# Eight more attention units transposed outside TensorE, and the whole instruction order as one list

## The chip, the cores and the metric

The kernel runs on one NeuronCore of one Trainium2 chip. The metric is the device time of one execution in microseconds (us), as a median of runs. The engines go by the profile's names: PE is TensorE (matmul), PEld its weight loads, DVE is VectorE, ACT is ScalarE, POOL is GpSimd, SP issues most of the DMAs. They share nothing but memory and semaphores; each runs its own instructions strictly in the order in which they stand in the program.

## What is computed

Banded attention with a linear bias, and behind it a layer whose activation is a ratio of two polynomials, all in float32 (8 batches, 8 heads, 576 positions, 64 numbers per head; 4608 tokens of 512 numbers, 2048 hidden numbers):

```python
scores = scale * np.matmul(q, k.transpose(0, 1, 3, 2))
...
mask = (rel >= 0) & (rel < window)          # window = 128
scores = np.where(mask, scores + bias[None], -1000000000.0)
scores = scores - np.max(scores, axis=-1, keepdims=True)
attn = np.exp(scores)
attn = attn / (np.sum(attn, axis=-1, keepdims=True) + 1e-09)
return np.matmul(attn, v)                   # becomes x
...
h = x @ w_in
P = a[0] + a[1] * h + a[2] * h2 + a[3] * h3
Q = 1.0 + np.abs(b[0]) * np.abs(h) + np.abs(b[1]) * h2
g = P / (Q + 1e-6)
return g @ w_out
```

## The kernel before

**The layer.** The 36 blocks of 128 tokens form 18 tiles of two blocks. A tile goes through the 16 chunks of 128 hidden numbers, two chunks at a time: the up matmuls (L980) fill one PSUM bank `h`, a chain on ACT, POOL and DVE (L1008 to L1026) turns `h` into `g`, split into a high part `g_h` (a cast on ACT) and the rest `g_l` (a subtraction on DVE, L1026, the last reader of `h`), and the down matmuls (L1044) add `g_h` and `g_l` times the weights into two banks `acc`. To keep float32 accuracy every product is made of three: high times high, low times high, high times low. So nearly all PE time is in six kinds of matmul. There are three `h` banks; an up group can start only when the bank that it takes has been released.

**The attention.** 76 units, each two heads and one or two blocks of a tile, four units for each later tile. A unit's matmuls stand in a *session* on PE between matmuls of the layer: the scores of unit u (L558), and the probabilities times `v` of unit u-2 (L694), whose result goes into two banks, `px` (one of the three banks that `h` uses too) and `py`. ACT then copies `px` away (`x<-px`, a copy that shows as line L387) and DVE adds `py` (L707); a cast and a subtraction (L709, on DVE or POOL) make `x_hi` and `x_lo`. Between scores and values stands the softmax: DVE (L567, L574), ACT (L579), POOL (L621). The values need the probabilities transposed, key by query. Two ways exist:

- *On PE*: `turn_halves` transposes them with eight matmuls (L604) at the head of the next session, three copies (L651, L652) bring them back to SBUF, and two affine selects on POOL (L658) cut them into the two sides of the band.
- *Through HBM*: `cross`: one DVE instruction (L629) transposes all the 32 by 32 squares of the 128 by 512 probabilities, one DMA writes them to HBM (`z_dram`), four DMAs read them back with the squares in their new places, and two affine selects on POOL (L636) cut them. Units from `CROSS` up to the last but two go this way.

**What sets the order.** Every piece of work is an `Op` with a due time, the engines that can run it and a cost. `Plan.order` puts them into one list: first the codes in `FIRST` one by one (number of the op, plus 10000 if its second possible engine is to run it), then a greedy choice among the ops that are ready by the plan's own estimate of times. The list is only an order: on the chip semaphores decide when each instruction starts. In the kernel before, `FIRST` has 1370 codes of 6486 ops; the greedy choice makes the rest, from about 60 us on.

Of the kernel before, what the change touches and what calls it, by code (L numbers as in the profile page):

```python
# [11 lines left out]
F32 = mybir.dt.float32  # L12
# [8 lines left out]
P = 128  # L21
# [318 lines left out]
def banded_attention_ratio_mlp(ctx: ExitStack, tc: tile.TileContext, kqv, w_in, w_out, ab, bias, ident, out):  # L340
# [22 lines left out]
    CROSS, CT, CM = 24, 2.27, 0.744  # L363
# [5 lines left out]
    def slot(pool, shape, dtype, name, tag=None, view=None):  # L369
        return Slot(pool, count[id(pool)], shape, dtype, name, tag or name, view)  # L370

    def ap(s):
        if s.ap is None:
            s.ap = s.pool.tile(s.shape, s.dtype, name=s.name, tag=s.tag)
        return s.ap
# [134 lines left out]
    class Unit:  # L510
# [112 lines left out]
        def cross(self):  # L623
            u, A, m, n, pr = self.u, self.A, self.m, self.n, self.pr
            z = slot(const, [P, 4, n, 32], F32, "z", tag=("spare0", "part")[u % 2])
            d = slot(dr4, [P, 4, n, 32], F32, "z_dram")
            x = slot(const, [P, 4, n, 32], F32, "x_turn", tag=("raw", "w1")[u % 2])
            w = self.w = slot(sb2, [P, 2, 4 * n, 32], F32, "p_all")
            plan.op(A + CT, {"v": 69 + 1.042 * n * P}, lambda e: nc.vector.transpose(ap(z).rearrange("q k y c -> q (k y c)"), ap(pr).rearrange("q y c -> q (y c)")), reads=[(pr, y) for y in range(n)], writes=[(z, 0)], follows=([*(y[0] for y in heads.values())], [parts[1]])[u % 2] if u < CROSS + 2 else (), sb=True)  # L629
            plan.op(A + CT, {"s": 728}, lambda e: eng[e].dma_start(ap(d), ap(z)), reads=[(z, 0)], writes=[(d, 0)])  # L630
            for k in range(4):
                r = slice(32 * k, 32 * k + 32)
                plan.op(A + CT, {"s": 182}, lambda e, k=k, r=r: eng[e].dma_start(ap(x)[r], ap(d)[:, k].rearrange("(g a) y c -> a g (y c)", a=32)), reads=[(d, 0)], writes=[(x, k)])
            cost = {"g": 135 + 0.93 * n * P}
            for k, sign in ((1, 1), (0, -1)):
                plan.op(A + CM - 0.1 * k, cost, lambda e, k=k, sign=sign: nc.gpsimd.affine_select(  # L636
                    out=ap(w)[:, k].rearrange("q (g y) c -> q g y c", g=4), in_=ap(x), pattern=[[32 * sign, 4], [0, n], [sign, 32]], compare_op=ALU.is_ge, fill=0.0, base=k - 1, channel_multiplier=-sign), reads=[(x, j) for j in range(4)], writes=[(w, k)])
# [73 lines left out]
    def attention(u):  # L711
# [25 lines left out]
        if u > CROSS and not turned:  # L737
            cost += 70
# [440 lines left out]
```

## Time and profile before

| what | value |
|---|---|
| three runs | 980.14, 982.7, 983.0 us; median 982.7 |
| the profiled execution's own time | 981.46 us |
| its span, first to last instruction | 979.7 us |
| granted TensorE clock, mean | 0.999 of 2.4 GHz |
| busy share: PE, PEld, DVE, ACT, POOL | 99%, 86%, 82%, 68%, 56% |
| mean DMA rate | 97 GB/s |

A busy PE says only that some matmul was under way: matmuls are pipelined, and each record (0.28 us for 256 columns) overlaps the next, which starts 0.12 us later. A stall shows best as the distance between the starts of two matmuls that follow each other.

### The profile page before, as it was taken

How to read it: one execution, taken by the hardware profiler on the slowest of the kernel's cores; microseconds unless marked ns; L12 is line 12 of the kernel's file. 1: busy time of each engine (PE TensorE's matmuls, PEld its weight loads, DVE VectorE, ACT ScalarE, POOL GpSimd, SP SyncE). 2: the span in 40 equal slices, each digit the busy share in tenths (PEclk: the TensorE clock that was granted, in tenths of full speed). 3: DMA queues.
4: the chain of work that ended last, by engine and by line, in shares of the span. 5: the costliest groups of instructions: out<-in, count | busy, mean ns of one | idle time of the engine just before them, and what ended most of it. 6: DMA issues, size and time to landing. Idle time of an engine off the chain costs nothing.

```text
span 979.7 us, 24224 instructions
## 1 busy us (share of the span) xinstructions
PE 971.1 (99%) x9029; PEld 840.7 (86%) x9031; DVE 806.6 (82%) x1929; ACT 666.8 (68%) x1567; POOL 549.3 (56%) x626
## 2 busy tenths in 40 slices
PE   9999999999999999999999999999999999999998
PEld 5767898888988888888888888888888888888997
DVE  5999988877878787978887888888887978886775
ACT  6999776676766666666666666666676666666563
POOL 3898965555655555645555454556555555454332
PEclk9999999999999999999999999999999999999999
DMA  8963212112323222323232322323232323210000
GB/s 278 364 234 127 90 52 67 44 66 71 114 93 124 68 96 87 115 73 103 96 103 85 108 94 78 125 67 120 84 101 79 114 79 99 73 53 23 1 23 22
DMA packets 81142, 95.30 MB, mean 97 GB/s; under 512 B 8448, under 2 KB 59264, under 8 KB 81024
## 3 DMA queue, kind: packets, MB, share of 16 engines
q1 hardware_dynamic: 80736, 93.49, 28.6%
q8 instruction: 71, 1.16, 0.5%
q14 instruction: 47, 0.39, 0.1%
q10 hardware_dynamic: 288, 0.26, 0.1%
HBM read 71.18 MB, written 22.54 MB: 96 GB/s over the span
## 4 chain that ended last, share of the span: by engine, by line
PE 87%; DVE 5%; DMA 3%; ACT 2%; issue 1%; SPq 1%; POOL 0%; ACTq 0%; DVEq 0%
PE h L980 39%; PE acc L1044 39%; PE sc L558 4%; PE px L694 3%; DMA raw_w<-in_w_in 2%; DMA kq<-in_kqv 1%; DVE g_p L1012 1%; DVE g_l L1026 1%; ACT g_p L1010 1%; DVE h L1018 1%; DMA raw_w<-in_w_out 1%; PE py L694 1%; DVE w L906 0%; ACT g_u L1008 0%; DVE g_q L1017 0%
## 5 line engine op out<-in xcount | busy, mean ns | idle before, releaser
L980 PE MATMUL h<-x_hi,wi_hi 128*128 128x256 f32 x1024 | 291.9, 285 | 2.4 <-DVE g_l L1026 2.3
L980 PE MATMUL h<-x_lo,wi_hi 128*128 128x256 f32 x1024 | 287.6, 281 | 0.0
L980 PE MATMUL h<-x_hi,w_lo 128*128 128x256 f32 x1024 | 287.3, 281 | 0.0
L1009 POOL TENSOR_SCALAR g_q<-g_u,babs 128x512 f32<-128x512 f32 x142 | 109.4, 770 | 216.9 <-ACT g_u L1008 211.8
L980 PEld LDWEIGHTS h<-x_lo,wi_hi 128*128 128x128 f32 x1024 | 192.6, 188 | 35.2
L1044 PE MATMUL acc<-wo_hi,g_h 128*128 128x512 f32 x548 | 221.8, 405 | 0.0
L980 PEld LDWEIGHTS h<-x_hi,wi_hi 128*128 128x128 f32 x1024 | 192.9, 188 | 33.4 <-issue 14.0
L1044 PE MATMUL acc<-w_lo,g_h 128*128 128x512 f32 x548 | 216.2, 395 | 0.0
L1044 PE MATMUL acc<-wo_hi,g_l 128*128 128x512 f32 x548 | 208.6, 395 | 0.0
L980 PEld LDWEIGHTS h<-x_hi,w_lo 128*128 128x128 f32 x1024 | 193.6, 189 | 0.0
L1011 POOL TENSOR_TENSOR g_q<-g_q,g_u 128x512 f32<-128x512 f32 x143 | 184.8, 1293 | 13.9 <-DVE g_q L1009 2.9
L1017 DVE SCALAR_TENSOR_TENSOR g_q<-g_q,h 128x512 f32<-128x512 f32 x144 | 98.5, 684 | 77.0 <-ACT h L1016 75.1
L1014 ACT ACTIVATE g_u<-g_q,guard 128x512 f32<-128x512 f32 x144 | 104.2, 724 | 81.8 <-POOL g_q L1011 81.8
L1008 ACT ACTIVATE g_u<-h 128x512 f32<-128x512 f32 x141 | 84.2, 597 | 82.0 <-PE h L980 81.9
L621 POOL TENSOR_TENSOR pr<-pr,st 128x512 f32<-128x512 f32 (+1 forms) x76 | 75.7, 996 | 107.9 <-DVE st L590 32.4
L387 ACT CAST g_h<-h 128x512 fp32r<-128x512 f32 x134 | 78.6, 586 | 69.1 <-DVE h L1024 62.7
L1012 DVE TENSOR_TENSOR g_p<-h,g_p 128x512 f32<-128x512 f32 x144 | 98.7, 685 | 30.7 <-ACT g_p L1010 30.2
L579 ACT ACTIVATE pr<-pr,st 128x128 f32<-128x128 f32 x288 | 113.5, 396 | 15.1 <-DVE st L574 12.2
L1044 PEld LDWEIGHTS acc<-wo_hi,g_h 128*128 128x128 f32 x548 | 103.1, 188 | 7.8 <-issue 1.2
L1026 DVE TENSOR_TENSOR g_l<-h,g_h 128x512 fp32r<-128x512 f32 x137 | 94.0, 686 | 17.8 <-ACT g_h L387 16.3
L1010 ACT ACTIVATE g_p<-h,na 128x512 f32<-128x512 f32 x140 | 108.6, 776 | 0.0
L1013 DVE SCALAR_TENSOR_TENSOR g_p<-g_p,na,h 128x512 f32<-128x512 f32 x144 | 106.8, 741 | 1.7
(112 smaller groups left out, 1761.3 us busy)
## 6 DMA issues: line engine op xcount, KB each, us to landing
kq<-in_kqv SPq DMA_DIRECT2D x68, 320.0 KB, 3.3
v<-in_kqv SPq DMA_DIRECT2D x68, 192.0 KB, 2.8
z_dram<-z SPq DMA_DIRECT2D x50, 256.0 KB, 2.0
x_turn<-z_dram SPq DMA_DIRECT2D x200, 64.0 KB, 2.0
out<-o SPq DMA_DIRECT2D x34, 256.0 KB, 2.0
raw_w<-in_w_in SPq DMA_DIRECT2D x16, 512.0 KB, 6.6
raw_w<-in_w_out SPq DMA_DIRECT2D x16, 512.0 KB, 6.2
bias_t<-in_bias SPq DMA_DIRECT2D x44, 64.0 KB, 2.4
```

The lines of the kernel that those rows point to most:

```text
L579: nc.scalar.activation(self.row(y), self.row(y), AF.Exp, bias=ap(st)[:, y : y + 1], scale=-1.0, accum_out=ap(st)[:, 4 + y : 5 + y])
L980: nc.tensor.matmul(h(i), w[:, k, :], x[:, k, :], start=(k == 0 and m == 0), stop=(k == NKC - 1 and m == len(seq) - 1))
L1008: plan.op(E, either(soon, act(W, 1), dve(W)), lambda e: nc.scalar.activation(v(g_u), v(h_s), AF.Abs) if e == "a" else nc.vector.tensor_sca ...
L1009: plan.op(E, {"g": tsc, "v": dve(W / 2, 1)} if soon else {"g": tsc}, lambda e: eng[e].tensor_scalar(v(g_q), v(g_u), ap(babs)[:, 1:2], ap(b ...
L1010: plan.op(E, either(soon, act(W, 1, 2) - 20, dve(W, 2)), lambda e: nc.scalar.activation(v(g_p), v(h_s), AF.Identity, bias=ap(na)[:, 2:3], ...
L1011: plan.op(E, {"g": ttc, "v": dve(W)} if soon else {"g": ttc}, lambda e: eng[e].tensor_tensor(v(g_q), v(g_q), v(g_u), ALU.mult), reads=[(g_ ...
L1012: plan.op(E, {"v": dve(W)}, lambda e: nc.vector.tensor_tensor(v(g_p), v(h_s), v(g_p), ALU.mult), reads=[(h_s, 0), (g_p, 0)], writes=[(g_p, ...
L1013: plan.op(E, {"v": dve(W, 1)}, lambda e: stt(v(g_p), v(g_p), ap(na)[:, 1:2], v(h_s), ALU.add, ALU.mult), reads=[(h_s, 0), (g_p, 0)], write ...
L1014: plan.op(E, {"a": act(W, 0, 1)}, lambda e: nc.scalar.activation(v(g_u), v(g_q), AF.Ln, bias=guard, scale=1.0), reads=[(g_q, 0)], writes=[ ...
L1017: plan.op(E, {"v": dve(W)}, lambda e: stt(v(g_q), v(g_q), GUARD, v(h_s), ALU.add, ALU.mult), reads=[(g_q, 0), (h_s, 0)], writes=[(g_q, 0)])
L1026: plan.op(E, {"v": dve(W)}, lambda e: nc.vector.tensor_tensor(v(g_l), v(h_s), v(g_h).bitcast(F32), ALU.subtract), reads=[(h_s, 0), (g_h, 0 ...
L1044: nc.tensor.matmul(ap(accs[n][i]), x[:, sl], w, start=(c == c0 and part == 0 and m == 0), stop=(c == c1 - 1 and (part == 1 or plain) and m ...
```

## The change

`CROSS` goes from 24 to 16, so units 16 to 23 take the way through HBM. The buffers of that way are laid out anew: the transposed squares and what comes back from HBM are now the two halves of one tile `turns`, in four buffers used in turn (before: two buffers for each of the two). And `FIRST` becomes a list of all 6510 ops: nothing is left to the greedy choice. Three costs that the plan reckons with change too; with a full list they decide nothing.

```diff
-    CROSS, CT, CM = 24, 2.27, 0.744
+    CROSS, CT, CM = 16, 2.27, 0.744
...
-            z = slot(const, [P, 4, n, 32], F32, "z", tag=("spare0", "part")[u % 2])
+            k = max(u - CROSS - 1, 0)
+            tag = ("spare0", "raw", "w1", "part")[k % 4]
...
+            both = slot(const, [P, 2, 4, n, 32], F32, "turns", tag=tag)
+            z, x = (lambda: ap(both)[:, 0]), (lambda: ap(both)[:, 1])
             d = slot(dr4, [P, 4, n, 32], F32, "z_dram")
-            x = slot(const, [P, 4, n, 32], F32, "x_turn", tag=("raw", "w1")[u % 2])
...
-            cost += 70
+            cost += 12
...
-    473, 488, 525, 280, 281, 260, 633, 351, 370, 520, 554, 489, 524, 490, 491, 457, 492, 371, 532, 274, 493, 475,
...
+    473, 488, 525, 280, 281, 260, 633, 351, 370, 520, 554, 489, 524, 490, 491, 457, 371, 522, 261, 458, 555, 268,
```

What the list does is seen where instructions stand. Lines of the changed kernel are 233 (up to `cross`) or 235 higher: L604 is L837, L558 is L791, L694 is L929, L980 is L1215, L1044 is L1279, L1026 is L1261, L567 is L800. A number behind a tile's name only tells buffers apart; the brackets name the semaphores that an instruction waits for (PE_49 those of PE, and so on).

PE at the head of the session of unit 19, before:

```order
L1044 MATMUL acc_2283<-wo_hi,g_l 128x512 [waits DVE_49]
L604 MATMUL px<-id_sb,pr 128x64 [waits PE_49,Pool_49]
L604 MATMUL sc_2329<-id_sb,pr 128x64
L604 MATMUL px<-id_sb,pr 128x64
L604 MATMUL sc_2329<-id_sb,pr 128x64
L604 MATMUL px<-id_sb,pr 128x64
L604 MATMUL sc_2334<-id_sb,pr 128x64
L604 MATMUL px<-id_sb,pr 128x64
L604 MATMUL sc_2334<-id_sb,pr 128x64
L558 MATMUL sc_2329<-kq 64x2x64 [waits DMAHW4_49]
```

and of the change:

```order
L1279 MATMUL acc_2248<-wo_hi,g_h 128x512 [waits DVE_49,Activation_49]
L1279 MATMUL acc_2248<-w_lo_1923,g_h 128x512
L1279 MATMUL acc_2248<-wo_hi,g_l 128x512 [waits DVE_49]
L791 MATMUL sc_2254<-kq 64x2x64 [waits DMAHW5_49]
L791 MATMUL sc_2256<-kq 64x2x64
```

The eight transposes, and their wait for POOL, are gone; the session begins with the scores. It is so in the eight sessions of units 17 to 24.

PE at the end of the session of unit 28 (the last values, then the layer), before:

```order
L694 MATMUL py<-p_all,v 64x64 x2
L1044 MATMUL acc_3762<-wo_hi,g_h 128x512 [waits Activation_49]
L1044 MATMUL acc_3762<-w_lo_911,g_h 128x512
L1044 MATMUL acc_3780<-wo_hi,g_h 128x512
L1044 MATMUL acc_3780<-w_lo_911,g_h 128x512
L980 MATMUL h<-x_hi,wi_hi 128x256 [waits DVE_49,PE_49]
L980 MATMUL h<-x_lo,wi_hi 128x256
```

and of the change:

```order
L929 MATMUL py<-p_all,v 64x64 x2
L1279 MATMUL acc_3780<-wo_hi,g_l 128x512
L1279 MATMUL acc_3749<-wo_hi,g_h 128x512
L1279 MATMUL acc_3749<-w_lo_820,g_h 128x512
L1215 MATMUL h<-x_hi,wi_hi 128x256 [waits Activation_49]
L1215 MATMUL h<-x_lo,wi_hi 128x256
```

Before, the first up matmul behind the session stands behind four down matmuls and waits for DVE (the `g_l` that releases its `h` bank); in the change it stands behind three and waits for ACT (the copy that releases the session's `px` bank). Over the last 50 sessions that have values, the first up group waits for DVE in 32 before and in 1 of the change, and for ACT in 5 before and in 39 of the change.

DVE at the same place, before:

```order
L1012 TENSOR_TENSOR g_p<-h,g_p 128x512
L567 COPY_PREDICATED sc_3897<-id_sb,sc_3897 128x2x128
L1026 TENSOR_TENSOR g_l<-h,g_h 128x512
L1013 SCALAR_TENSOR_TENSOR g_p<-g_p,na,h 128x512
L707 TENSOR_TENSOR x<-py,x 128x256
```

and of the change:

```order
L1247 TENSOR_TENSOR g_p<-h,g_p 128x512
L823 RECIPROCAL st<-st 128x4
L1248 SCALAR_TENSOR_TENSOR g_p<-g_p,na,h 128x512
L1261 TENSOR_TENSOR g_l<-h,g_h 128x512
L865 STREAM_TRANSPOSE turns<-pr 128x512
L800 COPY_PREDICATED sc_3852<-id_sb,sc_3852 128x2x128
```

Before, `g_l` stands behind the first DVE instruction of the new scores (L567); in the change it stands ahead of it. `g_l` stands directly behind L567 in 23 places before, and in 3 of the change. On DVE and POOL a few ops change engine as well: of the `x_lo` subtractions (L709) 15 run on DVE before and 7 in the change, the rest on POOL.

## Rows read from the trace of the kernel before

**Rows 1.** The page: span, busy time by engine, granted clock by slice.

```profile
span 979.7 us, 24224 instructions
...
PE 971.1 (99%) x9029; PEld 840.7 (86%) x9031; DVE 806.6 (82%) x1929; ACT 666.8 (68%) x1567; POOL 549.3 (56%) x626
...
PEclk9999999999999999999999999999999999999999
```

**Rows 2.** The page: the chain that ended last, by engine.

```profile
PE 87%; DVE 5%; DMA 3%; ACT 2%; issue 1%; SPq 1%; POOL 0%; ACTq 0%; DVEq 0%
```

**Rows 3.** Busy time by stretch of time, us from the start.

```profile
core 0: us, PE busy (x) PEld busy (x) DVE busy (x) ACT busy (x) POOL busy (x), PEclk, DMA share, GB/s
...
110.00:235.00 125.00, 125.00 (x1259) 111.18 (x1260) 105.01 (x256) 86.85 (x224) 77.41 (x91) 1.00 0.19 64
235.00:900.00 665.00, 662.64 (x6385) 585.70 (x6378) 551.25 (x1332) 445.17 (x1045) 359.48 (x398) 1.00 0.28 91
```

**Rows 4.** PE in order of time, a session with transposes: start, us, instruction.

```profile
136.33 0.40 PE L1044 MATMUL acc<-wo_hi,g_l 128*128 128x512 f32 x1
136.66 0.27 PE L604 MATMUL px<-id_sb,pr 64*128 64x64 f32 x1
...
137.05 0.94 PE L558 MATMUL sc<-kq 64*64 64x128 f32 x24
...
138.59 0.50 PE L1044 MATMUL acc<-wo_hi,g_l 128*128 128x512 f32 x1
```

**Rows 5.** PE in order of time, the session of unit 28, without transposes.

```profile
272.43 0.39 PE L1044 MATMUL acc<-wo_hi,g_l 128*128 128x512 f32 x1
...
274.13 0.22 PE L694 MATMUL px<-p_all,v 64*64 64x64 f32 x1
...
274.28 0.50 PE L1044 MATMUL acc<-wo_hi,g_h 128*128 128x512 f32 x1
```

**Rows 6.** All engines in order of time, behind that session.

```profile
274.38 0.38 ACT L387 COPY x<-px 128x256 f32<-128x256 f32 x1
...
274.53 0.42 DVE L567 COPY_PREDICATED sc<-id_sb,sc 128x256 f32<-128x256 uint32 x1
...
274.85 0.40 PE L1044 MATMUL acc<-wo_hi,g_h 128*128 128x512 f32 x1
274.86 0.68 DVE L1026 TENSOR_TENSOR g_l<-h,g_h 128x512 fp32r<-128x512 f32 x1
275.09 0.39 PE L1044 MATMUL acc<-w_lo,g_h 128*128 128x512 f32 x1
...
275.69 0.35 PE L980 MATMUL h<-x_hi,wi_hi 128*128 128x256 f32 x1 [0.22 <-DVE g_l L1026]
```

**Rows 7.** PE in order of time, behind the session of unit 71.

```profile
833.25 0.40 PE L1044 MATMUL acc<-w_lo,g_h 128*128 128x512 f32 x1
834.06 0.35 PE L980 MATMUL h<-x_hi,wi_hi 128*128 128x256 f32 x1 [0.41 <-DVE g_l L1026]
```

**Rows 8.** Groups by line: count, busy us, mean ns, idle before.

```profile
L629 DVE STREAM_TRANSPOSE z<-pr 128x512 f32<-128x512 f32 x50 | 35.6, 711 | 7.6 <-POOL pr L621 7.4
L658 POOL TENSOR_SCALAR_AFFINE_SELECT p_all<-p_all 128x512 f32<-128x512 f32 (+1 forms) x44 | 26.4, 600 | 9.2 <-ACT p_all L387 5.6 <-DVE o L1085 1.9 <-DVE p_all L387 0.2
L636 POOL TENSOR_SCALAR_AFFINE_SELECT p_all<-x_turn 128x512 f32<-128x512 f32 x100 | 70.3, 727 | 7.0 <-DMA x_turn<-z_dram 7.0
```

**Rows 9.** DMA issues: count, KB each, median us to landing.

```profile
z_dram<-z SPq DMA_DIRECT2D x50, 256.0 KB, 2.0
x_turn<-z_dram SPq DMA_DIRECT2D x200, 64.0 KB, 2.0
```

**Rows 10.** Instructions on the tile x: count, ns minimum/median/maximum, first and last start.

```profile
L387 ACT COPY x<-px x63: 350/376/412, 32.4 to 886.0; 128x256 f32<-128x256 f32 x63
...
L709 POOL TENSOR_TENSOR x_lo<-x,x_hi x47: 728/741/747, 117.0 to 888.6; 128x256 fp32r<-128x256 f32 x47
L709 DVE TENSOR_TENSOR x_lo<-x,x_hi x15: 417/1224/1236, 167.7 to 875.1; 128x256 fp32r<-128x256 f32 x15
```

More of the change, by code (lines that the diff above doesn't have):

```diff
@@ L624, in cross @@
             u, A, m, n, pr = self.u, self.A, self.m, self.n, self.pr
-            z = slot(const, [P, 4, n, 32], F32, "z", tag=("spare0", "part")[u % 2])
+            k = max(u - CROSS - 1, 0)
+            tag = ("spare0", "raw", "w1", "part")[k % 4]
+            before = {"spare0": [x[0] for x in heads.values()], "raw": [parts[0]], "w1": [w32[1]], "part": [parts[1]]}[tag] if k < 4 else []
+            both = slot(const, [P, 2, 4, n, 32], F32, "turns", tag=tag)
+            z, x = (lambda: ap(both)[:, 0]), (lambda: ap(both)[:, 1])
@@ L626, in cross @@
             d = slot(dr4, [P, 4, n, 32], F32, "z_dram")
-            x = slot(const, [P, 4, n, 32], F32, "x_turn", tag=("raw", "w1")[u % 2])
             w = self.w = slot(sb2, [P, 2, 4 * n, 32], F32, "p_all")
-            plan.op(A + CT, {"v": 69 + 1.042 * n * P}, lambda e: nc.vector.transpose(ap(z).rearrange("q k y c -> q (k y c)"), ap(pr).rearrange("q y c -> q (y c)")), reads=[(pr, y) for y in range(n)], writes=[(z, 0)], follows=([*(y[0] for y in heads.values())], [parts[1]])[u % 2] if u < CROSS + 2 else (), sb=True)
@@ L630, in cross @@
-            plan.op(A + CT, {"s": 728}, lambda e: eng[e].dma_start(ap(d), ap(z)), reads=[(z, 0)], writes=[(d, 0)])
+            plan.op(A + CT, {"v": 636}, lambda e: nc.vector.transpose(z().rearrange("q k y c -> q (k y c)"), ap(pr).rearrange("q y c -> q (y c)")), reads=[(pr, y) for y in range(n)], writes=[(both, "z")], follows=before, sb=True)
+            plan.op(A + CT, {"s": 728}, lambda e: eng[e].dma_start(ap(d), z()), reads=[(both, "z")], writes=[(d, 0)])
             for k in range(4):
                 r = slice(32 * k, 32 * k + 32)
-                plan.op(A + CT, {"s": 182}, lambda e, k=k, r=r: eng[e].dma_start(ap(x)[r], ap(d)[:, k].rearrange("(g a) y c -> a g (y c)", a=32)), reads=[(d, 0)], writes=[(x, k)])
@@ L634, in cross @@
-            cost = {"g": 135 + 0.93 * n * P}
+                plan.op(A + CT, {"s": 182}, lambda e, k=k, r=r: eng[e].dma_start(x()[r], ap(d)[:, k].rearrange("(g a) y c -> a g (y c)", a=32)), reads=[(d, 0)], writes=[(both, k)])
             for k, sign in ((1, 1), (0, -1)):
-                plan.op(A + CM - 0.1 * k, cost, lambda e, k=k, sign=sign: nc.gpsimd.affine_select(
-                    out=ap(w)[:, k].rearrange("q (g y) c -> q g y c", g=4), in_=ap(x), pattern=[[32 * sign, 4], [0, n], [sign, 32]], compare_op=ALU.is_ge, fill=0.0, base=k - 1, channel_multiplier=-sign), reads=[(x, j) for j in range(4)], writes=[(w, k)])
+                plan.op(A + CM - 0.1 * k, {"g": 680}, lambda e, k=k, sign=sign: nc.gpsimd.affine_select(
+                    out=ap(w)[:, k].rearrange("q (g y) c -> q g y c", g=4), in_=x(), pattern=[[32 * sign, 4], [0, n], [sign, 32]], compare_op=ALU.is_ge, fill=0.0, base=k - 1, channel_multiplier=-sign), reads=[(both, j) for j in range(4)], writes=[(w, k)])
```

313 rows, old and new, of the table FIRST are left out of this document.

## The prediction

> **What bounds the kernel now.** The page comes first: PE is busy for 971.1 of 979.7 us at the full clock [rows 1], and the chain that ended last is PE's for 87% [rows 2]. No other engine is near that: from 235 to 900 us DVE is busy for 83% of the stretch, ACT for 67%, POOL for 54% [rows 3]. So a change pays only if it takes matmuls off PE or closes gaps between them. A busy share of 99% hides small gaps, so I read PE in order of time. Two down matmuls that follow each other start 0.23 to 0.24 us apart (274.85 and 275.09 in [rows 6]); any more ahead of the next layer matmul is entry into or exit from a session, or a stall. Behind the session at 272.8 us, the last down matmul starts at 275.09 and the up matmul that follows it at 275.69: 0.60 us apart, 0.37 lost [rows 6]. The up matmul waits for `g_l`, which DVE ends at 275.54 (274.86 + 0.68), 0.15 us ahead of the matmul; DVE had L567 in front of it. Between 240 and 900 us I count fourteen such places, all behind sessions, from this first one to the last [rows 7], where 0.81 us lie between the two starts and 0.58 are lost. With 0.233 us taken off each, the fourteen sum to 4.6 us. That is all that a better order can win there; the rest is matmuls back to back.
>
> **The transposes.** In a session that has them, 0.39 us pass from the first transpose (136.66) to the first score matmul (137.05) [rows 4]. From the last layer matmul ahead to the first behind it are 2.26 us with transposes [rows 4] and 1.85 without [rows 5]: 0.41, which agrees. Eight sessions lose them: 8 x 0.39 = 3.1 us off PE. Nothing comes onto PE in exchange. This is the one certain term, since PE has no slack to hide it in.
>
> **What pays for it elsewhere.** Each of the eight units gives DVE one transpose, 8 x 0.71 = 5.7 us; its two affine selects on POOL go from 0.64 or less (0.60 is the mean over both sizes) to 0.73, some 2 us in all [rows 8]. ACT, and in a few cases DVE, loses three copies per unit. In the stretch concerned, 110 to 235 us, DVE is busy for 105.0 of 125 us [rows 3]; with 5.7 more it is at 89%, without what it gives up. That is cover enough if the work is spread; with none of it the price would be 5.7 us. I take nothing. The new DMAs, 5 per unit, land 2.0 us after issue [rows 9], in a stretch where the DMA engines are 19% busy [rows 3]. The values are needed two sessions later. With the PE matmuls of the new order added up at 0.118 and 0.233 us each, the shortest stretch between a unit's session and that in which its values stand is 18.0 us for units 16 on (before 15.3, and 18.5 to 18.7 for many units), so the round trip has about the room that it had. I take nothing for it; at worst all eight arrive late by one landing, 8 x 2.0 = 16 us.
>
> One rule speaks against this part. The probabilities cost PE 0.39 us a unit [rows 4] and will cost DVE 0.71 [rows 8] and a trip through HBM. The Trainium skill (VectorE: DVE Perf Modes, the section on the three transpose paths and the rules for kernel authors behind it) says that a VectorE transpose does only squares of 32 and that a full 128 by 128 one belongs on TensorE when PSUM will do as its target. By that rule the move is a loss, of 5.7 - 3.1 = 2.6 us if DVE set the pace. The rows side with the rule on the price of the operation, and against it on the engine that counts, as long as PE is the one without slack.
>
> **The order.** From the order of the instructions, the cause of the fourteen stalls is gone at nearly all places: of 50 sessions the first up group behind them waits for DVE in 1 in place of 32, and `g_l` stands directly behind the session's L567 in 3 places, not 23. The sessions are also spread more evenly: the matmuls between two of them add up, before, to a repeated 16.9, 11.3, 5.7 and 11.2 us; now most are 9 to 12.5. I take the whole 4.6 us as freed, with nothing freed as the other end.
>
> **The new wait.** 39 of these up groups now wait for the ACT copy of `px`. Its price by the rows: the session's last matmul ends at 274.35 (274.13 + 0.22) [rows 5], the copy starts at 274.38 and ends at 274.76 [rows 6]; with the 0.15 us that `g_l` took to release a matmul, the bank is free at 274.91. Behind three down matmuls (274.28, then two more starts, as in [rows 5, 6]) the up matmul would start at 275.09. So the copy may be 0.18 us late. Queued behind a waiting up matmul are all later down matmuls, that is everything. ACT instructions of this chain take some 0.6 us and ACT is 67% busy [rows 3], so if the copy meets ACT at random it is on average past its slack by 0.67 x 0.42 x 0.42 / (2 x 0.6) = 0.10 us; behind four matmuls (slack 0.41) by 0.02. There are 18 groups behind three, 10 behind four, 11 behind more: 18 x 0.10 + 10 x 0.02 = 2.0 us. The ends: 0, if ACT always stands ready as in [rows 6], and 18 x 0.42 + 10 x 0.19 = 9.5 if ACT has always just begun something. I take 2.0, nearer to the row.
>
> **The sum.** 981.46 (the profiled execution's own time, 1.76 over its span) - 3.1 - 4.6 + 2.0 = 975.8. The median of the three runs stands 1.24 above that execution, so in terms of the median 977.0.
>
> Eight of the `x_lo` subtractions go from DVE, where they take 0.42 us at best and 1.22 in the median, to POOL, where they take 0.74 [rows 10]. The Trainium skill (SBUF — State Buffer, section on who interferes with whom) has it that a VectorE instruction with two SBUF inputs and a GpSimd one that reads SBUF block each other for a whole instruction; the two durations on DVE agree with that. By it, DVE gains some 6 us over the kernel, which lies off PE's path and is not in the sum.
>
> **The rivals.**
> - *The stalls only move.* The first 55 us of the order are as before and the rest is as tight for other waits: up groups behind ACT, `acc` banks released with less room (the least PE work between the last use of an `acc` bank and the next is 0.94 us, before 1.30, against a copy of 0.6), sessions behind POOL. Then only the transposes count: 982.7 - 3.1 = 979.6. Speaks for it: a slack of 0.18 us is thin. Against: 4.6 us would have to come back in full.
> - *No gain.* The new waits eat transposes and freed stalls, 7.7 us in all, a price between my 2.0 and the end of 9.5: about 982.5.
> - *The copy of `px` is late throughout; slower.* With 39 up groups behind it, the kernel is slower by over 0.3% when they lose 3.1 + 4.6 + 2.95 = 10.65 us, 0.27 each beyond the slack: a copy that starts 0.45 us late on average. That is beyond what random meetings give (0.2 late on average: 0.67 x 0.3), but possible where ACT stands in front of it with something that itself waits. Time 986.
> - *DVE sets the pace from 110 to 235 us*, the rule's case: 982.7 - 3.1 + 5.7 = 985.3. Against it are 20 us of idle DVE in that stretch [rows 3].
>
> **How the numbers follow.** The forecast, 52%; the stalls only move, 25%; no gain, 13%; slower through the copy, 7%; slower through DVE, 3%. A difference of 0.3% (2.95 us of 982.7) is about what a measurement of this kernel can tell from none. The forecast is faster by more than that; 979.6 lies just at the bound, so that case is shared, 12 to 13; no gain counts as same; 985.3 lies just under the bound of 985.65, and I count it as slower, since PE would wait for more than the transposes alone. Faster 0.64, same 0.26, slower 0.10. The forecast's own range goes from 973.5 (no new waits, 975.0, less half of the 2.9 by which the runs of before lie apart) to 979.5; the range given reaches to the case of no gain: 972.5 to 983.
>
> **What the profile would show.** L604's successor has 32 matmuls in all, 64 fewer; PE's busy time falls by 4 to 8 us, the span to about 974. Up matmuls 0.6 us behind a down matmul, released by `g_l`, are gone; what is left shows ACT's copy as the releaser and mostly 0.1 to 0.3 us. DVE transposes count 58, reads back from HBM 232 with landings still near 2 us, and no session waits for POOL's affine selects. I am wrong if PE waits behind most sessions for the copy, if gaps appear between 60 and 235 us where the work was moved most, or if the new order holds `g_h` back so that down matmuls wait for ACT.

## The result and the profile after

The changed kernel takes 969.91 us (median of four runs, 968.84 to 971.38), the kernel before 981.93 (four runs, 980.14 to 983.0). The ratio is 0.988, with a 95% interval of 0.9858 to 0.9903: 12 us faster, about twice what was forecast, and 2.6 us below the lower end of the range. The profiled execution is the slowest of the four, 971.38 us with a span of 969.7. Line numbers are those of the kernel whose profile is shown, each run its own; an up matmul is known by its output `h`, a down matmul by `acc`.

The page: span, busy time, granted clock; and the chain that ended last. They answer to [rows 1, 2].

```profile
span 969.7 us, 24074 instructions
...
PE 961.8 (99%) x8965; PEld 839.7 (87%) x8967; DVE 789.7 (81%) x1876; ACT 653.6 (67%) x1548; POOL 567.4 (59%) x682
...
PEclk9999999999999999999999999999999999999999
...
PE 93%; DMA 3%; DVE 2%; issue 1%; SPq 1%; ACT 1%; DVEq 0%; ACTq 0%
```

PE has 64 matmuls less, as it must, but its busy time falls by 9.3 us, three times the 3.1 us that they took. PE's share of the chain goes from 87% to 93%; DVE's, from 5% to 2%. The time came out of places where PE waited. DVE does eight transposes more and is busy for 17 us less.

Busy time by stretch, for [rows 3]:

```profile
core 0: us, PE busy (x) PEld busy (x) DVE busy (x) ACT busy (x) POOL busy (x), PEclk, DMA share, GB/s
110.00:235.00 125.00, 125.00 (x1215) 111.13 (x1214) 109.22 (x258) 87.97 (x213) 82.40 (x97) 1.00 0.30 97
235.00:890.00 655.00, 655.00 (x6359) 586.65 (x6358) 532.78 (x1274) 431.15 (x1033) 370.37 (x443) 1.00 0.29 93
```

From 235 to 890 us PE is busy for 655.00 of 655 us; before, 2.36 us were missing between 235 and 900. In the stretch of the moved units DVE goes from 105.0 to 109.2 us, less than the 5.7 of the eight transposes.

What PE waited for over the whole execution, the five largest, in us, times, longest:

```profile
PE sc L791 <- DMA kq<-in_kqv: 0.9, 1, 0.9
PE sc L791 <- DVE w L1141: 0.9, 1, 0.9
PE warm L1335 <- PEq L1402: 0.8, 1, 0.8
PE px L1026 <- POOL p_all L893: 0.5, 2, 0.3
PE sc L837 <- DVE w L1141: 0.5, 1, 0.5
...
```

No up matmul (L1215) is in the list, neither behind `g_l` nor behind ACT's copy. All the waits of the list lie ahead of 74 us. What is gone is seen in single instructions behind the session of unit 28, which answers to [rows 5, 6] (PE, ACT and DVE in order of time):

```profile
270.88 0.43 DVE L800 COPY_PREDICATED sc<-id_sb,sc 128x256 f32<-128x256 uint32 x1 [0.82 <-PE sc L791]
...
271.28 0.22 PE L929 MATMUL py<-p_all,v 64*64 64x64 f32 x1
...
271.43 0.50 PE L1279 MATMUL acc<-wo_hi,g_l 128*128 128x512 f32 x1
271.53 0.37 ACT L620 COPY x<-px 128x256 f32<-128x256 f32 x1 [2.33 <-PE py L929]
...
272.00 0.39 PE L1279 MATMUL acc<-w_lo,g_h 128*128 128x512 f32 x1
272.23 0.28 PE L1215 MATMUL h<-x_hi,wi_hi 128*128 128x256 f32 x1
272.35 0.28 PE L1215 MATMUL h<-x_lo,wi_hi 128*128 128x256 f32 x1
```

The up matmul starts 0.23 us behind the last down matmul, and the next 0.12 behind it: nothing is lost. ACT had been idle for 2.33 us when the session ended; the copy begins 0.03 us behind the session's last matmul (271.28 + 0.22 = 271.50) and ends 0.33 us ahead of the up matmul. To sum up what is lost, I took the distances of all matmuls of the layer from 235 us on that follow each other directly, less 0.117 us behind an up matmul and 0.233 behind a down matmul, and summed what was over 0.02. Left out is the first distance behind a session, which is 0.1 us longer at 55 places in either kernel. Before: 31 places of a down and an up matmul, 8.4 us with the matmul behind each. After: one place, 0.02 us.

Groups, DMA issues and the instructions on `x`, for [rows 8 to 10]:

```profile
L865 DVE STREAM_TRANSPOSE turns<-pr 128x512 f32<-128x512 f32 x58 | 41.0, 707 | 5.8 <-POOL pr L854 5.1 <-issue 0.3
L871 POOL TENSOR_SCALAR_AFFINE_SELECT p_all<-turns 128x512 f32<-128x512 f32 x116 | 81.9, 727 | 22.1 <-DMA turns<-z_dram 10.4 <-PE h L1215 7.7 <-issue 1.3
...
turns<-z_dram SPq DMA_DIRECT2D x232, 64.0 KB, 2.0
...
L944 POOL TENSOR_TENSOR x_lo<-x,x_hi x55: 727/740/762, 120.1 to 897.2; 128x256 fp32r<-128x256 f32 x55
L944 DVE TENSOR_TENSOR x_lo<-x,x_hi x7: 415/417/593, 188.2 to 690.4; 128x256 fp32r<-128x256 f32 x7
```

The transposes cost what they cost before, and the way back from HBM still lands after 2.0 us. The seven `x_lo` left on DVE take 0.417 us in the median, not 1.22.

### The profile page after: what moved, and what is told of

Its sections match the earlier page's. It is cut to its first block, busy times and chain, and to the rows that moved or that the text cites. A ratio compares the mean times of both kernels' runs of the same rounds, so it can differ in the third digit from the quotient of the medians.

```text
span 969.7 us, 24074 instructions
## 1 busy us (share of the span) xinstructions
PE 961.8 (99%) x8965; PEld 839.7 (87%) x8967; DVE 789.7 (81%) x1876; ACT 653.6 (67%) x1548; POOL 567.4 (59%) x682
## 4 chain that ended last, share of the span: by engine, by line
PE 93%; DMA 3%; DVE 2%; issue 1%; SPq 1%; ACT 1%; DVEq 0%; ACTq 0%
PE acc L1279 42%; PE h L1215 40%; PE sc L791 5%; PE px L929 4%; DMA raw_w<-in_w_in 2%; DMA kq<-in_kqv 1%; DMA raw_w<-in_w_out 1%; PE py L929 1%; DVE w L1141 0%; PE px L1026 0%; DVE g_q L1252 0%; PE pt L830 0%; SPq L721 0%; ACT raw_w L1133 0%; DVE pr L807 0%
## 5 line engine op out<-in xcount | busy, mean ns | idle before, releaser
L1215 PE MATMUL h<-x_hi,wi_hi 128*128 128x256 f32 x1024 | 289.0, 282 | 0.0
L1215 PE MATMUL h<-x_lo,wi_hi 128*128 128x256 f32 x1024 | 287.8, 281 | 0.0
L1215 PE MATMUL h<-x_hi,w_lo 128*128 128x256 f32 x1024 | 287.4, 281 | 0.0
L1279 PE MATMUL acc<-wo_hi,g_h 128*128 128x512 f32 x548 | 220.5, 402 | 0.0
L1279 PE MATMUL acc<-w_lo,g_h 128*128 128x512 f32 x548 | 216.0, 394 | 0.0
L1215 PEld LDWEIGHTS h<-x_lo,wi_hi 128*128 128x128 f32 x1024 | 193.2, 189 | 21.2
L1215 PEld LDWEIGHTS h<-x_hi,wi_hi 128*128 128x128 f32 x1024 | 192.7, 188 | 16.1 <-issue 0.2
L1279 PE MATMUL acc<-wo_hi,g_l 128*128 128x512 f32 x548 | 206.1, 398 | 0.0
L1215 PEld LDWEIGHTS h<-x_hi,w_lo 128*128 128x128 f32 x1024 | 193.9, 189 | 0.0
L1261 DVE TENSOR_TENSOR g_l<-h,g_h 128x512 fp32r<-128x512 f32 x137 | 94.1, 687 | 30.8 <-ACT g_h L620 29.1
L1279 PEld LDWEIGHTS acc<-w_lo,g_h 128*128 128x128 f32 x548 | 103.4, 189 | 11.6 <-issue 0.5
L1279 PEld LDWEIGHTS acc<-wo_hi,g_h 128*128 128x128 f32 x548 | 103.2, 188 | 11.3 <-issue 1.9
L1279 PEld LDWEIGHTS acc<-wo_hi,g_l 128*128 128x128 f32 x548 | 100.8, 188 | 12.6 <-issue 0.2
```

The costliest lines, as they stand in the source:

```text
L1215: nc.tensor.matmul(h(i), w[:, k, :], x[:, k, :], start=(k == 0 and m == 0), stop=(k == NKC - 1 and m == len(seq) - 1))
L1261: plan.op(E, {"v": dve(W)}, lambda e: nc.vector.tensor_tensor(v(g_l), v(h_s), v(g_h).bitcast(F32), ALU.subtract), reads=[(h_s, 0), (g_h, 0 ...
L1279: nc.tensor.matmul(ap(accs[n][i]), x[:, sl], w, start=(c == c0 and part == 0 and m == 0), stop=(c == c1 - 1 and (part == 1 or plain) and m ...
```

## The experiments

All ratios are to the kernel before, on the same chip; its medians there were 981.8, 981.8 and 981.9 us.

**The changed kernel once more** (no edit).

> The changed kernel as it is, for a second profile and beside the others on one chip: 968 to 971.5. If the first 100 us differ from run to run by loads that land late (in the first profile a session waits 0.9 us for kq at 31 us and the first layer matmul comes 0.7 us later than before), this profile shows other waits there and the same gaps behind 110 us. If the waits come from the order, they are here again.

Measured: 969.68 us, ratio 0.9874 (0.986 to 0.9887); this execution spans 966.6 us. What PE waited for:

```profile
PE warm L1335 <- PEq L1402: 0.8, 1, 0.8
PE px L1026 <- POOL p_all L893: 0.5, 2, 0.3
PE sc L837 <- DVE w L1141: 0.4, 1, 0.4
...
PE sc L791 <- DMA kq<-in_kqv: 0.2, 1, 0.2
```

The 3.1 us between the two profiles lie in the first 110 us: from the 3160th-last up matmul (at 113 and at 110 us) to the end both need 856.74 us. The waits for `kq` and for a weight (`w`) ahead of that are 0.2 and 0.4 us instead of 0.9, 0.9 and 0.5, which is 1.7 of the 3.1. So what differs between these two executions is the start, with its loads, and a difference of this size there, between two profiles, says nothing of the change.

**The order behind 233 us.** The first 1634 instructions of the list (to about 233 us) as before, the other 4852 in the order of the change; two loads of `v` stand a few places later, where their buffer was not yet free. Beside the list, this is the edit against the changed kernel:

```diff
-    CROSS, CT, CM = 16, 2.27, 0.744
+    CROSS, CT, CM = 24, 2.27, 0.744
```

> 24 units transposed on PE as before (CROSS = 24), instructions up to about 233 us in the order of before, all the rest in the order of the change. Theory A (the order behind 235 us holds 8.7 us of stalls that the change lacks, whether or not the eight units are moved): 8 to 9 us faster, about 973, with at most 1 us lost at the seam. Rival B (the room comes from the eight units that left PE): 4 us faster or less.

Measured: 973.32 us, ratio 0.992 (0.9906 to 0.9935), 8.5 us faster than before. From 235 us on, two places are left, 0.3 us. Theory A holds. The kernel of this run also has the buffers of the change, four `turns` in place of two and two; these alone do not remove the stalls, since the next run has them too.

**The moved units, and the order up to 230 us.** The list of the change for the first 1662 instructions (about 230 us), the rest in the order of before; six loads stand a few places later. `CROSS` is 16.

> The change up to about 230 us (the eight units go through HBM, in the order of the change), all the rest in the order of before. Theory A: only the transposes count, 8 x 0.39 = 3.1 us, with up to 2 us either way from the first 100 us; about 979, and the stalls behind g_l from 235 us on are back (8 to 9 us of them). Rival B (the moved units make the room in which the stalls vanish): 973 or less. Rival C (DVE sets the pace once it has the eight transposes): 985.

Measured: 979.03 us, ratio 0.9969 (0.9956 to 0.9981), 2.8 us faster than before. The stalls are back, 8.2 us of them. PE in order of time at the first of them:

```profile
272.07 0.40 PE L1309 MATMUL acc<-wo_hi,g_h 128*128 128x512 f32 x1
272.31 0.39 PE L1309 MATMUL acc<-w_lo,g_h 128*128 128x512 f32 x1
272.92 0.35 PE L1245 MATMUL h<-x_hi,wi_hi 128*128 128x256 f32 x1 [0.22 <-DVE g_l L1291]
273.11 0.28 PE L1245 MATMUL h<-x_lo,wi_hi 128*128 128x256 f32 x1
```

0.61 us between the down and the up matmul where 0.23 are enough, and 0.19 to the next where 0.12 are. Theory A holds; rivals B and C do not. The two parts add up, 8.5 + 2.8 = 11.3 of 12.1 us; the rest is within the intervals.

**Eight transposes left in on PE.** In the sessions of units 17 to 24 of the changed kernel eight transposes of a constant are added, whose result nothing reads.

```diff
+        if CROSS < u <= CROSS + 8:
+            def again():
+                for n in range(4):
+                    for half in range(2):
+                        q = slice(Q * half, Q * half + Q)
+                        to = ap(sc[half])[:, 3 * P + n % 2 * Q :][:, :Q]
+                        nc.tensor.transpose(to, ap(id_sb)[q, 0, :], ap(id_sb)[q, 0, q], tile_position=(Q * half, 0))
+
+            emits.insert(0, again)
...
```

> The changed kernel with eight more matmuls of the transposes' form at the head of the sessions of units 17 to 24; they transpose a constant into unused columns of the score banks, so nothing reads them. All the rest stays as in the change. Theory A (the moved transposes are worth what they took on PE, 8 x 0.39 = 3.1 us, whatever the order): 3 us over the changed kernel, about 973. Rival (the new order has idle places that would have hidden them): under 1 us.

Measured: 973.75 us, ratio 0.9915 (0.9899 to 0.9931), 4 us over the changed kernel. In the trace the 62 sessions with values from 110 us on, taken from the start of the last layer matmul ahead to that of the first behind, sum to 112.91 us in place of 109.77: 3.14 more, 0.39 for each of the eight. From the 3160th-last up matmul to the end it is the same 3.14 us (859.87 in place of 856.74). Theory A holds; the rest of the 4 us lies ahead of that, where two executions of the changed kernel differ by 3.1 us.

**Twice the transposes on DVE**, for units 16 to 23 or for all 58. What is computed stays. The edit for the eight units (for all 58 the range is 2 throughout):

```diff
-lambda e: nc.vector.transpose(z().rearrange("q k y c -> q (k y c)"), ap(pr).rearrange("q y c -> q (y c)")), reads= ...
+lambda e: [nc.vector.transpose(z().rearrange("q k y c -> q (k y c)"), ap(pr).rearrange("q y c -> q (y c)")) for _ in range(2 if u < 24 else 1)], reads= ...
```

> The changed kernel, in which DVE does the transpose of units 16 to 23 twice: 8 x 0.7 = 5.7 us more on DVE between 130 and 235 us, where it is busy for about 87% of the time. Theory A (DVE has slack there): within 1 us of the changed kernel, about 970. Rival (DVE sets the pace once it transposes): up to 5.7 us more, 975.

> The same for all 58 units that go through HBM: 58 x 0.7 = 41 us more on DVE, which brings it from 81% to 86% of the span. Theory A (idle DVE time takes it up, and PE waits only where g_l or an accumulator's eviction now stands behind the second transpose): under 10 us over the changed kernel. Rival (what DVE gets more to do comes back on PE in large part): 20 us or more.

Measured: 969.08 us (0.9874, 0.986 to 0.9889) for the eight units, 969.66 us (0.9878, 0.9863 to 0.9894) for all. Neither differs from the changed kernel. The transposes and the stretches of the second:

```profile
L865 DVE STREAM_TRANSPOSE turns<-pr 128x512 f32<-128x512 f32 x116 | 82.3, 709 | 8.0 <-POOL pr L854 5.8
...
110.00:235.00 125.00, 125.00 (x1221) 111.43 (x1220) 114.99 (x267) 87.41 (x209) 82.78 (x97) 1.00 0.31 97
235.00:890.00 655.00, 655.00 (x6356) 586.50 (x6355) 564.41 (x1317) 431.37 (x1034) 370.22 (x443) 1.00 0.30 93
```

DVE is at 92% in the stretch of the moved units and at 86% behind, with 41 us of transposes that serve nothing, and PE has no gap from it. I had left room for 10 us; it cost none.

**ACT copies `px` twice.**

```diff
-lambda e: copy(e, both(), ap(bank)[:, col : col + 2 * P]), reads= ...
+lambda e: [copy(e, both(), ap(bank)[:, col : col + 2 * P]) for _ in range(2 if t >= 3 else 1)], reads= ...
```

> The changed kernel, but ACT copies px to x twice in a row in the sessions of the later tiles; the bank of px comes free about 0.51 us later (0.37 for the copy, 0.14 for the wait between the two). In the trace of the change the copy starts 0.03 us behind the last matmul of most sessions, and the up group behind three down matmuls starts 0.33 us after the copy ends. If the bank must be free 0.15 us ahead of the up matmul, 37 up groups are late by 9.4 us together, 12.2 with the 0.075 us of the matmul behind each. Theory A (the new wait costs nothing only because ACT always stands ready when a session ends): 979 to 982, that is 9 to 12 over the changed kernel, with ACT's copy as the releaser of the first up matmul in some 37 places. Rival (the copy has more room than that, or the up groups wait for something else): under 973.

Measured: 976.22 us, ratio 0.9947 (0.9933 to 0.9961), 6.5 us over the changed kernel: between the two theories. Behind the session of unit 28:

```profile
270.96 0.78 ACT L620 COPY x<-px 128x256 f32<-128x256 f32 x2 [2.33 <-PE py L929]
...
271.44 0.39 PE L1279 MATMUL acc<-w_lo,g_h 128*128 128x512 f32 x1
...
271.79 0.39 PE L1215 MATMUL h<-x_hi,wi_hi 128*128 128x256 f32 x1
...
272.01 0.28 PE L1215 MATMUL h<-x_lo,wi_hi 128*128 128x256 f32 x1
```

The two copies take 0.78 us, so the bank comes 0.41 later, not 0.51; and the up matmul starts 0.05 us behind their end (270.96 + 0.78 = 271.74), not 0.15. So the slack behind three down matmuls is 0.28 us, and 23 up groups from 110 us on stall by 0.12 to 0.29, 6.4 us in all with the matmul behind each. The mechanism of theory A is there; two of its sizes were wrong.

**`g_l` ahead of L567, in the order of before.** DVE at one of the 23 places:

```diff
 L1012 TENSOR_TENSOR g_p<-h,g_p 128x512
-L567 COPY_PREDICATED sc_3897<-id_sb,sc_3897 128x2x128
 L1026 TENSOR_TENSOR g_l<-h,g_h 128x512
+L567 COPY_PREDICATED sc_3897<-id_sb,sc_3897 128x2x128
 L1013 SCALAR_TENSOR_TENSOR g_p<-g_p,na,h 128x512
```

> The kernel before in its own order, written out as one list, with one edit: in the 23 places where g_l stands directly behind the first DVE instruction of the new scores (L567), g_l goes ahead of it. 21 of the 30 stalls that the trace of before has behind sessions from 235 us on are at such places; with the 0.075 us that the matmul behind a stalled one is late as well they hold 6.7 of 8.4 us. Behind the session of unit 28 g_l would end at about 275.21 in place of 275.54, which frees the up matmul within 0.05 us of its turn. Theory A (each stall is g_l being late, and goes with it): 5 to 6.5 us faster, about 976. Rival B (the stalls only move to the next wait, and the gain of the change comes from the even spread of the sessions): within 2 us of before.

Measured: 978.62 us, ratio 0.9963 (0.995 to 0.9976), 3.2 us faster: between the two theories. In the trace the stalls from 235 us on fall from 8.4 to 4.4 us. One that is left:

```profile
308.65 0.58 ACT L649 CAST g_h<-h 128x512 fp32r<-128x512 f32 x1
...
309.27 0.69 DVE L1288 TENSOR_TENSOR g_l<-h,g_h 128x512 fp32r<-128x512 f32 x1
...
309.73 0.40 PE L1306 MATMUL acc<-w_lo,g_h 128*128 128x512 f32 x1
...
310.11 0.35 PE L1242 MATMUL h<-x_hi,wi_hi 128*128 128x256 f32 x1
```

`g_l` now starts 0.04 us behind the end of `g_h` (309.23), the value that it needs, and the up matmul still comes 0.38 us behind the down matmul in place of 0.23. So L567 was about half of the cause. Of the 23 stalls left, 11 are of this kind and hold 2.5 us: there PE comes to the up group before the chain through `g_h` and `g_l` can be done, however DVE orders its work. At the other 12, 1.8 us, `g_l` starts 0.17 us behind the end of `g_h`, with the product `g_p` still in front of it on DVE.

**A later `g_l`, in both kernels.** DVE computes its first half once more ahead of the whole.

```diff
-lambda e: nc.vector.tensor_tensor(v(g_l), v(h_s), v(g_h).bitcast(F32), ALU.subtract), reads= ...
+lambda e: [nc.vector.tensor_tensor(v(g_l)[:, :x], v(h_s)[:, :x], v(g_h).bitcast(F32)[:, :x], ALU.subtract) for x in (W // 2, W)], reads= ...
```

> The changed kernel, in which DVE computes the first half of every g_l once more ahead of the whole (137 extra instructions on 128x256, about 0.4 us each, 57 us of DVE time): each g_l, and with it each release of an h bank by it, comes 0.4 to 0.55 us later. Theory A (the order of the change leaves room between each g_l and the up group that takes its bank, and that is why its stalls are gone, not because g_l and L567 swapped places): at most 4 us over the changed kernel, under 974. Rival B (the new order is only tight at other places, and what makes g_l late makes PE wait): 15 us or more over it.

> The same edit in the kernel before. Its 30 up groups behind sessions that wait for g_l already wait for it 0.147 us after its end, without any room. Theory A: each is later by 0.4 to 0.55 us, 12 to 16 us in all, and up groups that were just in time join them: 994 to 1000. Rival B (g_l is only the last of several things that these groups wait for): under 988.

Measured: the change with it 972.02 us (0.9893, 0.9879 to 0.9908), 2.3 over the changed kernel; the kernel before with it 985.71 us (1.0038, 1.0023 to 1.0052), 3.8 over before. In the change the gaps between layer matmuls from 110 to 950 us grow by some 0.2 us, those behind 950 us by 0.5, and one session waits for 0.5; from the 3160th-last up matmul to the end that is 1.1 us. Theory A holds there: the order leaves room for a `g_l` that is half a microsecond late. For the kernel before my number was far off: the time falls where rival B had it, under 988. Around the session of unit 28:

```profile
278.45 1.14 DVE L1026 TENSOR_TENSOR g_l<-h,g_h 128x256 fp32r<-128x256 f32 x2
...
278.68 0.39 PE L1044 MATMUL acc<-w_lo,g_h 128*128 128x512 f32 x1
...
279.74 0.35 PE L980 MATMUL h<-x_hi,wi_hi 128*128 128x256 f32 x1 [0.68 <-DVE g_l L1026]
```

This stall did grow, from 0.37 to 0.83 us lost. But of 31 places between a down and an up matmul only 13 are left from 235 to 950 us, mostly of 0.5 to 0.6 and about one for each 52 us, and the sum is 8.8 us, hardly more than 8.4. At 12 of the 13 the up matmul still starts 0.147 us behind the end of `g_l`, so there `g_l` is what it waits for; why the others are gone is open. Stalls of this kind are not independent. My reading of that, argued and not shown by a run of its own: one that is longer puts PE later against the chain, and the next up groups find their banks free. Of the 3.8 us, 0.4 are here, 1.8 in gaps from 95 to 235 us (2.5 in place of 0.7), and 1.3 in sessions that now wait.

## Why the prediction was right in sign and too small

**The transposes** were right: 8 x 0.39 = 3.1 us. The sessions with added transposes show 3.14, and the run with the moved units and the order up to 230 us gained 2.8.

**What pays for it elsewhere** was right to be taken as nothing, with more reserve than I gave it: doubling all 58 transposes on DVE is free. No session waits for the way through HBM. The Trainium skill (VectorE: DVE Perf Modes, the three transpose paths and the rules behind them) sends full 128 by 128 transposes to TensorE. The runs here do not bear that out for the time of the kernel: left on PE the eight cost 3 to 4 us, doubled on DVE nothing, because PE is the engine without slack and the four DMAs put the squares in their new places.

**The order** is the step that failed: "Between 240 and 900 us I count fourteen such places" and "That is all that a better order can win there". The mechanism, up matmuls that wait for `g_l` behind sessions, was right; the term was mis-sized: it measures 8.5 us, not 4.6. The fourteen were those over 0.15 us between a down and an up matmul, and they do sum to 4.6. Left out were 17 smaller ones at the same kind of place, 1.4 us, and behind each of the 31 the second up matmul, which starts 0.19 us after the first in place of 0.12: 2.4 us. 4.6 + 1.4 + 2.4 = 8.4. All but the last of the 31 up matmuls start 0.147 us behind the end of a `g_l`, so the releaser was right for the small ones too. The place of `g_l` behind L567 was only about half of why they were there, as the run with an early `g_l` shows; the rest of the order does the other half. Two parts of it come into question: the spacing of the sessions, which I had read from the order and given no term, and the bank that the first up group takes, which ACT's copy releases now and `g_l` released before. No run here separates the two.

**The new wait** was the second wrong term: 2.0 us were charged, 0 is measured. I let the copy meet ACT "at random". The new order keeps ACT free there: in most of the sessions the copy starts 0.03 us behind the last matmul, as it did in [rows 6]. The end of 0, which the row itself showed, was the likelier. Its slack is 0.28 us, not 0.18, since a copy on ACT releases PE 0.05 us after its end.

**The sum with the measured terms**: 981.8 (before, on the chips of the experiments) - 3.1 - 8.5 + 0 = 970.2, against 969.7 to 969.9. The offset of 1.24 us from the profiled execution to the median of three was noise: with all runs the median of before stands 0.3 to 0.5 above that execution.

**The rivals.** The stalls did not move: between layer matmuls PE has one gap of 0.02 us, and no larger one, from 110 to 950 us. DVE does not set the pace. The price of a late copy is real, 6.5 us for 0.41 us more in 58 sessions, but it takes a copy that is late; in the change none is.

**What the profile would show**: 32 transposes left on PE, 58 on DVE, 232 reads back, landings at 2 us and no session that waits for POOL's selects are as said. PE's busy time fell by 9.3 us where I said 4 to 8, for the reason above. What was said to be left, up groups that wait 0.1 to 0.3 us for ACT's copy, is not there at all.

**`x_lo`**, which was not in the sum: the DVE time of this group falls from about 14 to 3 us. Six of the seven left on DVE now take 0.42 us, their shortest time. The Trainium skill (SBUF — State Buffer, who interferes with whom) would explain the 1.22 us of before by POOL at work at the same time. The traces fit that: before, each of the ten that took 1.22 us or more began 0.35 us into a POOL product of 1.29 us (`g_q`, L1011) and ended 0.28 us behind it, while none of the five of 0.42 began with more than 0.08 us of a POOL instruction still to run; in the change the only longer one, 0.59 us, began inside a POOL select and ended 0.26 us behind it. No run varies it by itself. In neither trace does a matmul of the layer wait for `x_lo`.

## What to carry to other kernels

When an engine is at 99%, sum its lost time from all distances between instructions that follow each other, against the shortest distance of each kind: a threshold on single gaps and a look at the first late instruction alone missed nearly half of it here. A wait that a new order adds is charged by whether the releasing engine is free at that moment, which a row of the same kind shows, not by its average load. And a price per stall times the number of stalls is no forecast: with every `g_l` half a microsecond later it gave 12 to 16 us here, and 3.8 were measured.

## What was not expected of the hardware

- Behind a stall the second matmul is late too: the first up matmul after a wait is recorded with 0.35 us and the next starts 0.19 us later, where 0.28 and 0.12 are usual.
- An up matmul starts 0.147 us behind the end of a DVE instruction that releases its bank, but 0.05 us behind an ACT copy that does.
- Two executions of the same kernel differ by 3.1 us in their first 110 us alone, and by 0.01 us in the 857 us behind.
